# Half-size products for the first feed-forward matrix in 15 of 18 blocks, one pair's score seats from pair 10 on, and TensorE transposes for the first four pairs

## The chip, the core and the metric

The kernel runs on one core of a Trainium2 chip. The metric is the device time of one execution in microseconds (us). Engines: PE is TensorE (matmuls), PEld its weight loads, DVE VectorE, ACT ScalarE, POOL GpSimd, SP the engine that issues most DMAs. A matmul multiplies a stationary operand (`lhsT`, the weights, loaded by PEld) with a moving one (`rhs`) and writes to PSUM. A float32 matmul stands in the trace as two passes, each a weight load and a MATMUL, so the instruction counts of the profile are twice those of the program.

## The reference, cut to what matters

```python
# q, k, v: (8 batches, 8 heads, 576, 64); tau a scalar
scores = scale * q @ k.T
scores = where(scores >= max(scores) - tau, scores, -1e9)
attn = exp(scores - max(scores)); attn = attn / (sum(attn) + 1e-9)
x = (attn @ v), heads side by side            # (4608 tokens, 512)
h = x @ w_in                                  # (512 x 2048)
g = h * sigmoid(1.702 * h)
out = g @ w_out                               # (2048 x 512), float32
```

## The kernel before

**Attention.** Two heads make a pair `n`; there are 32 pairs, four to a batch. `load_qk` and `load_v` bring a pair in by DMA, `prep` (L504) turns q and k on DVE. `scores` (L514) makes nine tiles of 64 keys on PE, in bursts of four 64x64 quadrants; `keep` (L531) copies each from PSUM on ACT; `in_groups` (L537) takes maxima of groups on DVE, `over_tiles` and `over_halves` join them, and a row of thresholds is spread over the partitions, from most pairs by a DMA through DRAM (`turn_rows`, `row_out` L630, `row_in` L639; `BY_DMA` names the pairs), else by DVE (`spread_max` L618). Then, tile after tile, `sub` (L645, DVE), `mask` and `exps` (L651, L655, ACT). `values` (L666, PE) multiplies with v; the sums of the exponentials come from PE for the first five pairs (`sums_by_pe`) and from `in_groups` with an addition for the rest, their reciprocals again over DRAM (`turn_sums`, `sums_out`, `sums_in`). `place_x` (L768, DVE) scales the result into `xT`, the transposed input of the feed-forward part. The score tiles of a pair keep their place in SBUF (their seats) from `keep` to `values`; there are seats for two pairs, `s_m` and `s_t`. From pair 8 on (`JOINT = 7`, counted from 0) `values` of pair n-2 and `scores` of pair n alternate on PE tile by tile in one run, each new tile taking the seat that the old one leaves.

**Feed-forward.** 18 blocks of 256 tokens. Blocks 1 and 2 (`PLAIN = 2`) are done plainly together (`mm1_0` L823, `mm2` L805). In blocks 3 to 14 `mm1` (L783) makes the first product in 64 matmuls of 128x128 weights by 256 columns; `tanh` (L792, ACT) and `gelu` (L795, DVE) follow; the second product is made of seven half-size products instead of eight (`product` L974), with operand sums on POOL (`s_sums`, `s_last`) and seven results joined by DVE (`read` L996). Blocks 15 to 18 (`TAIL`) go two at a time through `two_blocks`: there the first product also is seven half-size products (`product1` L888: 112 matmuls of 256 columns for two blocks), read out by DVE (`read1` L904) into `hs`, and the weight sums (`w_sum` L862) are made on DVE and POOL when all pairs are placed.

**Order.** No hardware queue decides the order: `task` records every operation with its engine, a cost, a rank, what it comes after and which buffers it takes and gives; `run_in_order` plays these tasks through a list scheduler while the program is built and emits each engine's instructions in that order, which is then fixed. Pairs have low ranks and go on PE as soon as they are ready; feed-forward tasks (`LAST`) fill the rest. Pair n may not start before feed-forward task 16(n-6) has run:

```python
        gate = per_pair * (n - LEAD)
        ...
        after = [ffn[gate]] if gate >= 0 and ffn else []
```

`EARLY`, `SECOND`, `LATER` and `CV` are offsets added to the ranks. PSUM: `psA` has three slots of two banks (scores, values, and the odd products of `two_blocks`), `psM` two single banks (feed-forward).

Of the kernel before, what the change touches and what calls it, by code (L numbers as in the profile page):

```python
# [21 lines left out]
P = 128  # L22
# [10 lines left out]
def kernel(  # L33
# [84 lines left out]
    minus = const.tile([P, 2, KT], FP32, name="minus")  # L118
    own_row = const.tile([P, QB // 2], FP32, name="own_row")
# [8 lines left out]
    limits = {"psA": 3, "psM": 2, "s_m": 8, "s_t": 2, "io": 2, "hs": 2, "osb": 2, "xT": NXT, "mb": 1,  # L128
              "raw0": 1, "raw1": 1, "qkT0": 1, "qkT1": 1, "v_m0": 1, "v_m1": 1, "w64_0": 1, "w64_1": 1, "row": 1, "row_s": 1, "rc": 1}
    for x in ("raw0", "raw1", "qkT0", "qkT1", "mb"):  # L130
# [6 lines left out]
        "exps": 11.43,  # L137
        "in_groups": -31.63,
        "keep": -11.23,
        "load_qk": 20.14,  # L140
        "load_v": 19.9,
        "mask": 171.06,
        "one_row": -45.66,
        "over_halves": -1.59,
        "over_tiles": -20.68,
        "place_x": -28.05,
        "prep": -4.32,
        "row_in": 9.72,
        "row_out": -14.48,
        "scores_run": -28.58,  # L150
        "spread_max": 3.58,
        "spread_sums": 14.71,
        "sub": 178.85,
        "sums_by_pe": 312.21,
        "turn_rows": -14.38,
        "values": -19.56,
        "w_sum": -20.0,
    }
    SECOND = {
        "exps": 6.76,  # L160
        "in_groups": 291.18,
        "keep": 29.15,
        "load_qk": 165.77,
        "load_v": 335.03,
        "mask": 337.17,
        "one_row": -25.48,
        "over_halves": -20.33,
        "over_tiles": 311.35,
        "place_x": 0.09,
        "prep": -16.41,  # L170
        "row_in": 205.66,
        "row_out": 181.09,
        "scores_run": 21.47,
        "spread_sums": -6.66,
        "sub": 17.25,
        "sums_by_pe": 334.76,
        "sums_in": -21.09,
        "sums_out": 5.24,
        "turn_rows": 184.92,
        "turn_sums": -18.91,  # L180
        "values": -19.14,
    }
    LATER = {
        "exps": 208.23,
        "in_groups": 342.52,
        "keep": -7.99,
        "load_qk": 197.24,
        "load_v": -11.46,
        "mask": 344.07,
        "over_halves": -19.6,  # L190
        "over_tiles": 19.84,
        "place_x": 181.51,
        "prep": 208.92,
        "row_in": -6.54,
        "row_out": -30.86,
        "scores_run": -0.21,
        "sub": 200.03,
        "sums_in": 338.15,
        "sums_out": 7.27,
        "turn_rows": 167.17,  # L200
        "turn_sums": 343.8,
        "values": -25.3,
        "x_sum": -9.1,
    }
    CV = {
        "cv_end": 5.42,
        "cv_low": -24.3,
        "cv_power": 173.78,
        "cv_power2": -24.9,
        "cv_round": -14.9,  # L210
        "cv_whole": -11.38,
        "load_w": 330.13,
# [123 lines left out]
    TWICE = ()  # L336
# [12 lines left out]
    for tag, size, bufs in (  # L349
        ("s_m", 2 * S, 8), ("s_t", S, 2), ("raw0", S, 1), ("raw1", S, 1), ("qkT0", S, 1),  # L350
        ("qkT1", S, 1), ("mb", S, 1), ("rc", S, 1), ("v_m", NK * 2 * D, 2),
    ):
        room[tag] = [(end + x * size, size) for x in range(bufs)]
        end += bufs * size
# [12 lines left out]

    def seat_scores(n, t):

        if t < NKT and n in APART:  # L370
            return home(n, "s_m", f"s_m{t}")
        if n >= JOINT:
            tag, o, size = held[n, t] = held.pop((n - 2, t))
            return arena2[:, o : o + size]
        tag = "s_m" if t < NKT else "s_t"
        o, size = room[tag].pop(0)
        held[n, t] = tag, o, size
        return arena2[:, o : o + size]
# [13 lines left out]
    def load_qk(n, which, queue, h):  # L392
        b, hp = divmod(n, NPAIR)
        src = (q, k)[which]
        t = home(n, f"raw{which}")
        blocks = t.rearrange("p (c d) -> p c d", d=32)
# [7 lines left out]
        raws[n, which] = t  # L404

    def load_v(n):
        b, hp = divmod(n, NPAIR)
        t = seat("v_m", n % 2).rearrange("p (h j d) -> p h j d", j=NK, h=2)
        for h in range(2):
            for c in range(2):  # L410
                nc.sync.dma_start(
                    out=t[ts(c, KT), h],
                    in_=v[b, 2 * hp + h].rearrange("(k j) d -> k j d", k=KT),
                )
        vs[n] = t
# [90 lines left out]

    def halves(ap):
        return ap.rearrange("p (c s) -> p c s", c=2)

    def scores(n, j):  # L510
# [8 lines left out]
        if j == NK - 1 and n not in TWICE:  # L519
            del mats[n, 0], mats[n, 1]  # L520
# [12 lines left out]
    def in_groups(n, t, op):  # L533

        if (n, op) not in stats:
            stats[n, op] = work.tile([P, NK * QB], FP32, name="part", tag="part", bufs=2)
# [6 lines left out]
    def over_tiles(n, op):  # L543

        r = work.tile([P, QB], FP32, name="red", tag="red", bufs=2)
# [7 lines left out]
    def over_halves(n):  # L553
# [7 lines left out]
        if n in TWICE:  # L561
            for x, y in ((0, 0), (1, 2), (2, 1), (3, 3)):
                nc.vector.scalar_tensor_tensor(
                    out=flat[0][ts(y, 32), 0:QB], in0=r[ts(x, 32)], scalar=gap[ts(x, 32)],
                    in1=o[ts(x, 32)], op0=ALU.subtract, op1=ALU.max,
                )
            return
# [14 lines left out]

    def row_blocks(n):

        nc.vector.transpose(out=flat[1], in_=flat[0])
        mb = home(n, "mb")[:, 0:SH]
        nc.vector.tensor_tensor(
            out=mb.rearrange("p (g i) -> p g i", i=32),
            in0=flat[1].unsqueeze(1).to_broadcast([P, QB // 2, 32]),
            in1=own_row.unsqueeze(2).to_broadcast([P, QB // 2, 32]), op=ALU.mult,  # L590
        )
        mbs[n] = mb

    def again(n, j):
        ps = psA.tile([P, 2, 512], FP32, name="ps", tag="ps")
        for first in (True, False):
            for h in range(2):
                for c in range(2):
                    if first:
                        left = mats[n, 1][ts(h, D), ts(j, KT)]  # L600
                        right = mats[n, 0][ts(h, D), ts(c, SH)]
                    else:
                        left, right = minus[ts(h, D), c, :], mbs[n][ts(h, D), :]
                    nc.tensor.matmul(
                        ps[ts(c, KT), h, 0:SH], lhsT=left, rhs=right, start=first, stop=not first,
                    )
        if j == NK - 1:
            del mats[n, 0], mats[n, 1]
        pss[n, j] = ps

    def mask_one(n, j):
        nc.scalar.activation(
            out=sT[n, j // 2][:, j % 2], in_=pss.pop((n, j))[:, :, 0:SH], func=AF.Prelu, alpha=STEEP
        )
# [122 lines left out]
    def sums_in(n):  # L737
        rc, row = seat("rc"), rcs.pop(n)
# [7 lines left out]
    def spread_sums(n):  # L746
# [3 lines left out]
        rc = seat("rc")  # L750
# [77 lines left out]
    def gelu_0(j):  # L828
# [8 lines left out]
    TAIL = NBLK - 4  # L837
    WQ = NDC // 2 * HF * P
    gx_o = 4 * WQ
    xs_o = gx_o + N_G  # L840
    hs_o = xs_o + 3 * NDC // 2 * BLK
    assert hs_o + 8 * BLK <= end and BLK == 2 * P
    wc = [arena2[:, ts(x, WQ)].rearrange("p (c f) -> p c f", f=HF * P) for x in range(4)]
    gs = [g, arena2[:, ds(gx_o, N_G)].rearrange("p (f j t) -> p f j t", f=2, t=BLK)]
    xsum = [
        arena2[:, ds(xs_o + x * 2 * BLK, 2 * BLK)].rearrange("p (c t) -> p c t", c=2)
        for x in range(3)
    ]
    hs = [
        arena2[:, ds(hs_o + x * 4 * BLK, 4 * BLK)].rearrange("p (f h t) -> p f h t", f=2, h=2)  # L850
        for x in range(2)
    ]
# [3 lines left out]
        (wc[0], wq[1][0], wq[1][1], ALU.add), (wc[1], wc[0], wq[0][0], ALU.subtract),  # L856
        (wc[2], wq[0][0], wq[1][0], ALU.subtract), (wc[3], wq[0][1], wc[1], ALU.subtract),
    ]

    def w_sum(x, k, engine):  # L860
        o, a, b = (y[:, :, ts(k, 2 * P)] for y in W_SUMS[x][:3])
        engine.tensor_tensor(out=o, in0=a, in1=b, op=W_SUMS[x][3])  # L862

    def x_quarter(blk, d, h):
        return xTs[blk + h][:, ts(d, 2), :]
# [7 lines left out]

    BANK_OF = ("psA", "psM", "psA", "psM", "psA")
    places = {}

    def product1(blk, j, x):
        b11, b12, b21, b22 = (x_quarter(blk, d, h) for d in range(2) for h in range(2))
        left, right = (
            (wq[0][0], b11), (wq[0][1], b21), (wc[1], xsum[1]), (wc[2], b12),  # L880
            (wq[1][1], xsum[2]), (wc[0], xsum[0]), (wc[3], b22),
        )[x]
        if BANK_OF[(7 * j + x) % 5] == "psA":
            places[j, x] = psA.tile([P, 2, 512], FP32, name="ps", tag="ps")[:, 0, 0:BLK]
        else:
            places[j, x] = psM.tile([P, BANK], FP32, name="ops", tag="mo")[:, 0:BLK]
        for c in range(2):
            nc.tensor.matmul(  # L888
                places[j, x], lhsT=left[:, c, ts(j, P)], rhs=right[:, c, :],
                start=(c == 0), stop=(c == 1),  # L890
            )

    def read1(j, x):
        (c11, c12), (c21, c22) = ([hs[j % 2][:, f, h, :] for h in range(2)] for f in range(2))
        ps = places.pop((j, x))
        if x == P1:
            nc.scalar.copy(out=c21, in_=ps)
            return
        sums = {
# [585 lines left out]
```

## Time and profile before

| what | us |
|---|---|
| median of 3 runs (1298.23 to 1299.97) | 1299.56 |
| the profiled execution, its time | 1299.66 |
| its span, first to last instruction | 1297.9 |
| PE busy within the span | 1252.3 |
| DVE / ACT / POOL busy | 986.2 / 677.7 / 240.6 |

The span is the time between the first and the last instruction of the profiled execution; 1.8 us of its time lie outside it. Busy is the union of an engine's instructions; a row of instructions that overlap counts the overlap once. The prediction below reads the profile in stretches, since the kernel has a start (first loads and weight conversion), a long middle in which attention and feed-forward alternate, and a tail of feed-forward alone from about 1078 us on.

### The profile page before, as it was taken

To read this page: it belongs to the slowest core of one execution; us is meant where nothing else is said; L and a number is where in the kernel's file an instruction comes from. 1 tells how busy PE (TensorE), PEld (TensorE's weight loads), DVE (VectorE), ACT (ScalarE), POOL (GpSimd) and SP (SyncE) were. 2 spreads that over 40 slices of the span, in tenths; PEclk is the share of its full clock that TensorE was granted. 3 is DMA by queue.
4 is the path that set the end of the run, shared out by engine and by line. 5 is a ranking of instruction groups with operands and counts; after the bars stand their busy time and mean duration, and the time that the engine had idled before them with its cause. 6 is when DMAs were issued, how large, how long until landed. Compare 5 with 4: busy or idle time off the path is not lost. (4 is left out here: it accounts for less than half of the span.)

```text
span 1297.9 us, 22745 instructions
## 1 busy us (share of the span) xinstructions
PE 1252.3 (96%) x9128; PEld 972.9 (75%) x9128; DVE 986.2 (76%) x1553; ACT 677.7 (52%) x878; POOL 240.6 (19%) x277
## 2 busy tenths in 40 slices
PE   4689999999999999999999999999999999999998
PEld 2347854577777888777777788887777788888887
DVE  6999987989988787777887878777778863652642
ACT  5999876686755545454555555544546540210210
POOL 1000101131030303021120312030302117120120
PEclk8799999999999999999999999999999999999999
DMA  9735356183222222222122222222221100000000
GB/s 243 179 76 146 109 132 115 58 144 84 72 55 56 56 72 56 72 47 64 55 48 63 47 63 56 72 56 73 55 61 35 51 27 17 1 1 33 1 1 33
DMA packets 190825, 87.01 MB, mean 67 GB/s; under 512 B 159872, under 2 KB 170112, under 8 KB 190720
## 3 DMA queue, kind: packets, MB, share of 16 engines
q1 hardware_dynamic: 182560, 78.08, 23.7%
q0 software_dynamic: 5792, 7.19, 3.1%
q8 instruction: 71, 1.16, 0.4%
q10 hardware_dynamic: 2368, 0.30, 0.2%
q14 instruction: 34, 0.28, 0.1%
HBM read 71.63 MB, written 9.70 MB: 63 GB/s over the span
## 5 line engine op out<-in xcount | busy, mean ns | idle before, releaser
L537 DVE TRANSPOSE_TENSOR_REDUCE part<-arena 128x36 f32<-128x1152 f32 (+1 forms) x295 | 358.1, 1236 | 48.1 <-ACT arena L531 38.2
L783 PE MATMUL hps<-xT,w_in 128*128 128x256 f32 x1536 | 338.9, 381 | 2.9 <-DVE arena L795 2.9
L783 PEld LDWEIGHTS hps<-xT,w_in 128*128 128x128 f32 x1536 | 291.8, 191 | 48.9 <-issue 5.3
L651 ACT ACTIVATE arena<-arena 128x1152 f32<-128x1152 f32 (+1 forms) x160 | 169.4, 1059 | 127.4 <-DVE arena L645 127.2
L531 ACT COPY arena<-ps 128x576 f32<-128x576 f32 x288 | 171.0, 642 | 111.8 <-PE ps L514 108.9
L645 DVE TENSOR_TENSOR arena<-arena 128x1152 f32<-128x1152 f32 (+1 forms) x158 | 202.1, 1320 | 19.2 <-DMA arena<-row 19.1
L974 PE MATMUL ops<-w_out,arena 128*128 128x256 f32 x896 | 202.7, 381 | 1.7 <-DVE arena L795 1.6
L655 ACT ACTIVATE arena<-arena,shift,scl 128x1152 f32<-128x1152 f32 (+1 forms) x160 | 200.1, 1250 | 4.0
L974 PEld LDWEIGHTS ops<-w_out,arena 128*128 128x128 f32 x896 | 169.1, 190 | 29.4 <-DVE arena L795 3.8
L514 PE MATMUL ps<-arena 64*64 64x288 f32 x2304 | 172.1, 413 | 19.5 <-DVE neg L1035 9.1
L940 POOL TENSOR_TENSOR arena<-arena 128x256 f32<-128x256 f32 x56 | 51.8, 925 | 647.1 <-DVE arena L795 544.0
L666 PE MATMUL pv<-arena 64*64 64x288 f32 x2176 | 159.6, 407 | 0.0
L974 PE MATMUL ops<-arena 128*128 128x256 f32 x672 | 150.6, 380 | 0.0
L792 ACT ACTIVATE th<-hps 128x512 f32<-128x512 f32 x112 | 66.1, 590 | 161.7 <-PE hps L783 148.2
L514 PEld LDWEIGHTS ps<-arena 64*64 64x64 f32 x2304 | 85.4, 135 | 81.5 <-ACT arena L531 17.5
L974 PEld LDWEIGHTS ops<-arena 128*128 128x128 f32 x672 | 127.3, 190 | 19.3 <-issue 2.2
L666 PEld LDWEIGHTS pv<-arena 64*64 64x64 f32 x2176 | 81.0, 133 | 54.7 <-issue 8.8
L996 DVE SCALAR_TENSOR_TENSOR osb<-ops,osb 128x256 f32<-128x256 f32 x98 | 39.6, 415 | 94.2 <-PE ops L974 88.0
L795 DVE SCALAR_TENSOR_TENSOR arena<-th,hps 128x512 f32<-128x512 f32 x96 | 64.3, 670 | 37.4 <-ACT th L792 37.0
L908 ACT ACTIVATE th<-arena 128x512 f32<-128x512 f32 x32 | 20.3, 635 | 72.6 <-DVE arena L904 72.6
L953 POOL TENSOR_TENSOR arena<-arena 128x512 f32<-128x512 f32 x28 | 37.4, 1340 | 106.7 <-PE ops L974 106.6
L805 PE MATMUL ops<-w_out,arena 128*128 128x512 f32 x128 | 56.8, 598 | 0.0
(118 smaller groups left out, 1072.8 us busy)
## 6 DMA issues: line engine op xcount, KB each, us to landing
arena<-in_v_dram SPq DMA_DIRECT2D x128, 144.0 KB
arena<-in_q_dram SPq DMA_DIRECT2D x128, 72.0 KB
out_dram<-osb SPq DMA_DIRECT2D x36, 256.0 KB
arena<-in_k_dram SPq DMA_DIRECT2D x124, 72.0 KB
arena<-row SPq DMA_DIRECT2D x48, 144.0 KB
arena<-row_s SPq DMA_DIRECT2D x48, 144.0 KB
w_out<-in_moe_w_in_dram SPq DMA_DIRECT2D x12, 512.0 KB
arena<-in_moe_w_out_dram SPq DMA_DIRECT2D x12, 512.0 KB
```

The costliest lines, as they stand in the source:

```text
L514: nc.tensor.matmul(ps[ts(c, KT), h, 0:SH], lhsT=mats[n, 1][ts(h, D), ts(j, KT)], rhs=mats[n, 0][ts(h, D), ts(c, SH)], start=True, stop=True,)
L531: nc.scalar.copy(out=sT[n, t][:, u], in_=pss.pop((n, j))[:, :, 0:SH])
L537: nc.vector.tensor_reduce(out=stats[n, op][:, t * 2 * QB : min(2 * t + 2, NK) * QB], in_=sT[n, t].rearrange("p u h (g d) -> p (u h g) d", ...
L645: engine.tensor_tensor(out=s, in0=s, in1=mbs[n].unsqueeze(1).to_broadcast(list(s.shape)), op=ALU.subtract)
L651: nc.scalar.activation(out=s, in_=s, func=AF.Prelu, alpha=STEEP)
L655: nc.scalar.activation(out=s, in_=s, func=AF.Exp, scale=scl, bias=shift)
L666: nc.tensor.matmul(o[c][ts(h, D), 0:SH], lhsT=left(j, h)[ts(c, KT)], rhs=sT[n, t][ts(c, KT), u, h, :], start=(j == 0), stop=(j == NK - 1),)
L783: nc.tensor.matmul(hidden[j][:, ts(f, BLK)], lhsT=w_in[:, c, ds((f * HF + j) * P, P)], rhs=xTs[blk][:, c, :], start=(c == 0), stop=(c == N ...
L792: nc.scalar.activation(out=ths[j], in_=hidden[j], func=AF.Tanh, scale=GELU_SCALE / 2)
L795: nc.vector.scalar_tensor_tensor(out=g[:, :, j, :], in0=two(ths.pop(j)), scalar=1.0, in1=two(hidden.pop(j)), op0=ALU.add, op1=ALU.mult,)
L805: nc.tensor.matmul(acc[i], lhsT=g0[:, j, ts(i, P)], rhs=w_out[:, j, :], start=(j == 0), stop=(j == NFC - 1),)
L974: nc.tensor.matmul(banks[blk][k][:, ts(o, HM)], lhsT=left[:, j, :], rhs=right[:, j, :], start=(j == 0), stop=(j == HF - 1),)
```

## The change

1. **First product.** `FIRST7 = 3`: blocks 4 to 18, each by itself, make the first product of seven half-size products (`seven`). A half-size product has 128 tokens as its moving operand. Sums of partial products are kept in PSUM: P6, P7 and P4 accumulate on P1's bank, P3 on P5's; ACT copies the bank out between them (`keep1`), DVE adds P2, P5 and P3 to the copies (`add1`). Block 3 alone still uses `mm1`. `two_blocks`, `read1`, `hs` and the second copy of `g` are gone. The weight sums are made in the middle of the kernel (`w_sums`): ACT copies one operand (`w_copy`), a POOL DMA adds the other (`w_plus`).
2. **Seats.** From pair 10 on (`SINGLE = 9`) there are seats for one pair only; the other half of the arena holds the weight sums and `xsum`. `values` of pair n-1 and `scores` of pair n alternate, and `keep` waits also for the additions of the pair before.
3. **Thresholds.** `BY_DMA` ends at pair 9; from pair 10 on `spread_max` spreads them on DVE.
4. **First four pairs.** q and k are loaded in longer rows and turned by PE (`turn_in`), then copied from PSUM by ACT (q) and DVE (k).
5. All rank offsets differ, and each load has one of its own (`L_RANK`); the POOL sums of the second product go in halves of 512 columns, the subtraction (`s_minus`) apart.

```diff
-    BY_DMA = (0, 1, *range(3, NP))
+    BY_DMA = (0, 1, *range(3, SINGLE))
...
+    SINGLE = 9
+    TURNED = (0, 1, 2, 3)
...
+    def ahead(n):
+        return n - 1 if n >= SINGLE else n - 2
...
+        if n in TURNED:
+            rows = src[b, 2 * hp + h]
+            if which:
+                queue.dma_start(out=t[ts(h, D), :], in_=rows.rearrange("(k j) d -> k (j d)", k=KT))
+                return
+            queue.dma_start(
+                out=t[:, 0 : 4 * P].rearrange("p (c d) -> p c d", d=P)[:, :, ts(h, D)],
+                in_=rows[0 : 4 * P].rearrange("(c p) d -> p c d", p=P),
+            )
+            queue.dma_start(out=t[ts(h, D), 4 * P : S], in_=rows[4 * P : S])
+            return
...
+    def turn_in(n, which):
+        raw = raws.pop((n, which))
+        bank = pss[n, -1 - which] = psA.tile([P, 2, 512], FP32, name="ps", tag="ps")
+        ps = bank.rearrange("p a b -> p (a b)")
+        x = 0 if which else 4 * P
+        for o in range(0, x, P):
+            nc.tensor.transpose(ps[:, ds(o, P)], raw[:, ds(o, P)], eye)
+        for o in range(x, S, D):
+            for h in range(2):
+                nc.tensor.matmul(
+                    ps[ts(h, D), ds(o, D)], lhsT=raw[ts(h, D), ds(o, D)],
+                    rhs=eye[ts(h, D), ts(h, D)], start=True, stop=True,
+                )
...
-    TAIL = NBLK - 4
+    FIRST7 = 3
...
+    W_SUMS = [
+        (wc[0], wq[1][1], wq[1][0], 1.0), (wc[1], wc[0], wq[0][0], -1.0),
+        (wq[1][0], wq[0][0], wq[1][0], -1.0), (wc[2], wq[0][1], wc[1], -1.0),
+    ]
...
+    def w_copy(x, c):
+        o, _, b, sign = W_SUMS[x]
+        nc.scalar.activation(out=o[:, c, :], in_=b[:, c, :], func=AF.Copy, scale=sign)
+
+    def w_plus(x):
+        o, a = W_SUMS[x][:2]
+        nc.gpsimd.dma_start(out=o, in_=a, accum_op=ALU.add)
...
     def x_quarter(blk, d, h):
-        return xTs[blk + h][:, ts(d, 2), :]
+        return xTs[blk][:, ts(d, 2), ts(h, HT)]
...
+        o = bank1(x, y)
+        for j in range(4):
+            for c in range(2):
+                nc.tensor.matmul(
+                    o[:, ts(j, HT)], lhsT=left[:, c, ts(4 * y + j, P)], rhs=right[:, c, :],
+                    start=(x in (P1, P2, P5) and j + c == 0), stop=(j + c == 4),
+                    skip_group_check=True,
+                )
...
+    def keep1(x, y):
+        f, h = {P1: (0, 0), P6: (0, 1), P7: (1, 1)}[x]
+        nc.scalar.copy(out=quarter(y, f, h), in_=four(bank1(x, y)))
+
+    def add1(x, y):
+        f, h = {P2: (0, 0), P5: (1, 1), P3: (0, 1)}[x]
+        o = quarter(y, f, h)
+        nc.vector.tensor_tensor(out=o, in0=four(bank1(x, y)), in1=o, op=ALU.add)
...
+    def seven(blk):
...
+        for x in (P1, P2, P6, P5, P7, P4, P3):
+            for y in range(2):
...
+                if x in (P6, P7, P4):
+                    after = after + [keeps[{P6: P1, P7: P6, P4: P7}[x], y]]
+                if x == P3:
+                    after = after + [adds[P5, y]]
+                ffn.append(task(
+                    "PE", FFU, LAST, product1, blk, x, y, after=after,
+                    take=("psM",) if x == P1 else ("psA",) if x in (P2, P5) and y == 0 else (),
+                    give=("xT",) if x == P3 and y else (),
+                ))
...
         def copied(n, r, j, a):
-            copies.append(task("ACT", 0.55, r, keep, n, j, after=[a] + copies[-1:], give=("psA",)))
+            before = sumsd[n - 1][j // 2 :][:1] if n >= SINGLE else []
+            copies.append(task(
+                "ACT", 0.55, r, keep, n, j, after=[a] + copies[-1:] + before, give=("psA",)
+            ))
```

## The prediction

> **What bounds the kernel now.** I read the page's busy line and chain first, then the span in four stretches, the waits of PE, and single passes in the timeline of PE.
>
> ```profile
> PE 1252.3 (96%) x9128; PEld 972.9 (75%) x9128; DVE 986.2 (76%) x1553; ACT 677.7 (52%) x878; POOL 240.6 (19%) x277
> ...
> PE 17%; DVE 0%; issue 0%
> ```
>
> PE is busy in all but 45.6 us, and the chain that ended last is PE alone. By stretches (PE, PEld, DVE, ACT, POOL busy; then the granted clock):
>
> ```profile
> 0.00:108.60 108.60, 71.21 (x1009) 39.19 (x1009) 93.06 (x147) 91.77 (x121) 9.09 (x33) 0.91 0.64 157
> 108.60:260.00 151.40, 151.40 (x1035) 96.03 (x1032) 134.35 (x214) 116.60 (x155) 18.43 (x30) 1.00 0.45 115
> 260.00:1078.30 818.30, 813.84 (x6093) 648.39 (x6092) 664.10 (x1004) 442.81 (x550) 166.31 (x169) 1.00 0.26 61
> 1078.30:1298.00 219.70, 215.84 (x999) 189.35 (x997) 94.68 (x191) 26.56 (x53) 46.74 (x46) 1.00 0.03 13
> ```
>
> 37.4 of the 45.6 idle us lie before 108.6, where the feed-forward part starts; from there on PE waits 8.3 us in 1189. So work taken from PE after 108.6 comes off the end, as long as nothing else gets in its way. The waits agree: those on ACT's exponentials and on the turned q and k are in the start.
>
> ```profile
> PE den L666 <- ACT arena L655: 17.9, 8, 13.4
> PE ps L514 <- DVE neg L1035: 9.1, 1, 9.1
> PE ps L514 <- DVE arena L504: 6.1, 1, 6.1
> ...
> PE hps L783 <- DVE arena L795: 2.9, 2, 2.2
> ```
>
> **The first product.** A pass of 256 columns costs PE 32 passes from 607.47 to 614.38, 216 ns each (the row's mean of 380 overlaps):
>
> ```profile
> 607.47 7.07 PE L974 MATMUL ops<-arena 128*128 128x256 f32 x32
> 614.38 3.62 PE L974 MATMUL ops<-w_out,arena 128*128 128x256 f32 x16
> ```
>
> Removed: 704 matmuls of L783 (768 less the 64 of block 3) and all 224 of L888, two passes each: 1856 x 0.216 = 400.9 us. Added: 15 blocks x 14 tasks x 8 = 1680 matmuls of 128 columns, 3360 passes. None like it is in the trace. From below it costs half of 216, 108 ns. From above, 192: a weight load of 128x128 stands as 190 ns, begins 2 ns after the pass before it, and no pass could be shorter if it had to be over. Which end is nearer, one late load tells:
>
> ```profile
> 362.34 0.63 PE L783 MATMUL hps<-xT,w_in 128*128 128x256 f32 x2
> ...
> 362.49 0.19 PEld L783 LDWEIGHTS hps<-xT,w_in 128*128 128x128 f32 x1 [0.17 <-DVE arena L795]
> ...
> L783 PE MATMUL hps<-xT,w_in x7: 379/379/414, 361.5 to 362.8; 128*128 128x256 f32 x7
> ```
>
> This load waited for DVE and began 0.15 us after the pass at 362.34. The pass behind it lasted 414 instead of 379, so it was 35 ns late and in effect began 216 + 35 = 251 ns after 362.34: some 100 ns after its load began, not 190. A load therefore is about hidden under a half-size pass. I take 109 ns: 3360 x 0.109 = 366.2. Net **-34.7** (-38.0 at 108, +244 at 192).
> By the Trainium skill (TensorE: Matmul & The Clock Gate, Back-to-back issue gap), a stream of weight load and matmul pairs at 128 columns runs at about 81 ns a matmul where an isolated one takes 56, 25 ns more; an estimate by it is 3360 x 0.025 = 84 us on top, 1361 in all. This speaks against the change; the trace shows nothing of the kind at 256 columns, and no run here yet shows 128.
>
> **The middle: PE against DVE.** The program's order on PE is fixed when it is built, and in the middle it now repeats two gaps between the runs of `values` and `scores`: 208 short passes and 14 long (25.7 us), then 98 long and 16 short (22.9). With two runs of 8.9 (591.55 to 600.46) a cycle of two pairs and one block takes PE 66.4 us; before it was 73. DVE in that time:
>
> ```profile
> 473.00:546.00 73.00, 73.00 (x543) 58.68 (x543) 57.31 (x88) 38.43 (x49) 13.14 (x14) 1.00 0.24 57
> ...
> L795 DVE SCALAR_TENSOR_TENSOR arena<-th,hps 128x512 f32<-128x512 f32 x96 | 64.3, 670 | 37.4 <-ACT th L792 37.0
> L904 DVE TENSOR_TENSOR arena<-ps,arena 128x256 f32<-128x256 f32 x68 | 27.5, 421 | 15.9 <-PE ps L888 15.0
> L913 DVE SCALAR_TENSOR_TENSOR arena<-th,arena 128x512 f32<-128x512 f32 x32 | 25.5, 800 | 2.6 <-ACT th L908 2.6
> L618 DVE STREAM_TRANSPOSE arena<-red 128x576 f32<-128x576 f32 x1 | 0.8, 778 | 0.0
> ```
>
> Three such windows mean 58.0 us. Off it goes the block's share, 8 `gelu` x 0.67 and 7 `read` x 0.40 = 8.2, times 32/31 blocks: 49.6 for two pairs. Thresholds on DVE add per pair 0.78 (L618) and two more `fold` at 0.28 and one joining operation at 0.24, and drop two at 0.30 and `turn_rows` at 0.21: +0.8. A block now needs 6 `add1` (512 columns; between L795's 0.67 and twice L904's, 0.84; I take 0.67, the same size), 6 `gelu` out of SBUF at 0.80, 2 at 0.67, 4 `x_sum` at 0.41 (the 256-column `place_x`), 7 `read`: 14.6. Together 51.2 + 14.6 = 65.8 of 66.4 us. DVE goes from 79% to 99%, and nearly level with PE. The trace bears 98% for 65 us, from 292 to 357, with PE never waiting:
>
> ```profile
> 292.10:324.50 32.40, 32.40 (x334) 23.20 (x327) 31.59 (x55) 20.57 (x29) 5.62 (x5) 1.00 0.34 84
> 324.50:357.00 32.50, 32.50 (x254) 25.78 (x254) 32.27 (x45) 23.38 (x28) 2.00 (x4) 1.00 0.28 72
> ```
>
> I take 97% as what DVE can reach: 65.8 / 0.97 = 67.8, 1.4 us over PE in each of 10.5 cycles: **+14** (0 to +52, below). With one set of seats a run also waits for the last exponential of the pair before. From a run's start: last full maximum 10.2 (L537 ends 601.7), then `place_x` 0.9, tail 0.7, joining 1.8, spreading 0.8, first `sub` 1.4, four tiles at 2.44 on ACT (39.00 to 41.44 to 43.88) and a tail of 1.5: 27.1. In the short gap's 31.8 this has 4.7 to spare. In the long gap ACT's order puts four `keep1` and two `tanh` at 0.6 within the chain and DVE's two `add1` and a `gelu`: 32.7 of 34.6. What is late first is `add1` of P3: it frees the `psA` slot for the next run, and behind it on PE stands that whole run. `keep`'s new wait (sums of the pair before, DVE) holds the other copies on ACT and through `psA` the scores; the sums are over before it, since DVE does them first.
>
> **The start.** q and k of four pairs came in rows of 128 bytes (72 KB a DMA, 576 rows, two a head and operand: 18432 packets, of 22462 in the first 60 us); now 256 bytes for q, 2304 for k, some 5100. Thresholds of pair 1 took from 20.5 to 37.0 to return, against 5 us later on (606.5 to 611.6). Eight `prep` (0.72) leave DVE, four copies join DVE and four ACT (0.64); ACT also has about 0.7 more of conversion before the feed-forward part. The turns, 16 of 128 columns (0.109 to 0.43 each) and 160 small passes (at most 0.06 each, the 64x288 row), 3 to 17 us of PE, lie under 37.4 idle us; without that cover they would cost that much. ACT was idle 16.8 us of 108.6; that is the most that can come forward, and its 3.3 extra us the loss if nothing does. I take **-4** (-17 to +3).
>
> **Weight sums and queues.** `w_sums` puts eight ACT copies (1.04 each, the 128x1024 row) and four POOL DMAs of 1 MB (9 to 10 us to land, as L934) into 250 to 330. The four like DMAs at L934 came with 2.9 us of waits of PE there; I take **+2** (0 to +6). SP loses 92 issues for thresholds (L630, L639: 96 to 4) and POOL none; POOL's sums are as many columns as before. Second product and tail are four blocks of 48.6 us PE each as before (L974 unchanged, two blocks 24.2 + 24.2 in L888 against 48.8), under DVE's 14.6 a block.
>
> **Sum.** 1297.9 - 34.7 - 4 + 14 + 2 = 1275.2; with the 1.8 outside the span **1277**. The profiled execution (1299.66) is within 0.1 of the median, so it needs no correction.
>
> **Rivals.**
> - *No lag, quicker start.* DVE's 99% is too high since it counts operations that waited at 60 ns more than dense ones (two L537 take 2.63, one alone 1.38); the start gives 10. 1297.9 - 34.7 - 10 + 1 + 1.8 = **1256**.
> - *Some lag more*, 2.5 to 3.5 us a cycle: 1289 to 1299.
> - *DVE and the single seats set the pace.* POOL slows DVE (`sub` means 1.42 where most last 1.35), the long gap's DVE work, summed in its order up to P3's `add1`, is 36.4 us from the run's start against PE's 34.6, and PE can't use the short gap's slack since its order is fixed. At 5 us a cycle +52: **1315**, slower. It decides from 3.5 us on ((34.7 + 4 - 2) / 10.5). For it: the sums above; against it: 98% without a wait at 292 to 357.
> - *The weight load shows* in short passes, halfway to 192: 3360 x 0.041 = 138 more, **1415**; from 116 ns on nothing is gained. For it: the 190 of the rows. Against it: the late load. The rule quoted above is of this kind.
>
> **How the numbers follow.** Forecast 0.55 (own range 1264 to 1289), quicker 0.17, more lag 0.09, DVE's pace 0.13, weight load 0.06. 0.2%, 2.6 us, is what a measurement of this kernel can tell. Faster: 0.55 + 0.17 + 0.06 of the more-lag case = 0.78; same 0.04, where the two lag cases meet 1299.6; slower 0.12 + 0.06 = 0.18. The range leaves out a part of the quick case below (0.05), and above most of the DVE case (0.09) and the weight load (0.06): 1254 to 1305.
>
> **What would show it.** In the profile after: rows of 128 columns on PE in x16 pieces 1.74 us apart; PE busy near 1225 us; the first `mm1_0` pass at about 104; DVE at 95% or more from 300 to 1000; PE waits on L902 or on `ps` by one to two us a cycle. The prediction is wrong in its first step if short passes start 116 ns or more apart, in its second if PE waits more than 3 us a cycle or not at all.

## The result and the profile after

The changed kernel takes 1342.31 us (median of 4 runs, 1340.58 to 1346.92) against 1299.3 for the kernel before on the same chip: 1.0333 times, 95% interval 1.0315 to 1.0351. It is slower by 43 us where 1277 was forecast. The profiled execution took 1346.92, with a span of 1345.1.

The busy line and the chain of the page of after:

```profile
PE 1257.9 (94%) x10808; PEld 1013.1 (75%) x10808; DVE 1041.2 (77%) x1592; ACT 730.8 (54%) x964; POOL 212.1 (16%) x189
...
PE 52%; DVE 28%; ACT 9%; DMA 6%; issue 4%; POOL 1%; SPq 0%; DVEq 0%; ACTq 0%; POOLq 0%
```

Now 28% of the span goes through DVE and 9% through ACT: PE is no longer the only bound. (The chain of the kernel before held PE alone, but could be followed back over 17% of its span only; that PE was the bound there rests on its 8.3 idle us after 108.6.) The same four stretches as in the prediction, cut at the same events (start of the feed-forward part, end of the first two blocks, last `values`); columns as there:

```profile
0.00:113.10 113.10, 82.17 (x1185) 47.72 (x1185) 91.15 (x139) 92.93 (x125) 8.08 (x25) 0.86 0.58 146
113.10:271.80 158.70, 151.00 (x965) 93.66 (x962) 140.36 (x228) 119.20 (x155) 18.50 (x30) 0.98 0.47 117
271.80:1140.90 869.10, 825.17 (x7314) 685.41 (x7312) 750.36 (x1126) 485.00 (x626) 144.70 (x102) 0.99 0.24 54
1140.90:1345.00 204.10, 199.54 (x1356) 186.36 (x1352) 59.34 (x101) 33.72 (x60) 40.82 (x32) 1.00 0.04 14
```

In the third stretch PE stands idle for 44 us, in a stretch where it had been idle for 4.5. What it waited for there, by the waits of PE (total us, times, longest):

```profile
PE ops L970 <- DVE osb L992: 24.8, 10, 5.3
PE den L657 <- ACT arena L646: 17.3, 3, 11.8
PE ps L545 <- ACT arena L562: 9.4, 6, 6.6
PE ps L883 <- DVE arena L902: 6.3, 8, 0.8
```

The second and most of the third line belong to the start and to the first two blocks. The first line is new: the second product (`product` L970) waits for DVE to read the bank it is to write again (`read` L992).

The half-size product itself does nearly what was forecast. In PE's timeline 32 passes of 128 columns start 3.58 us before the next 32, 111.7 ns each:

```profile
584.74 3.74 PE L883 MATMUL ps<-xT,w_in 128*128 128x128 f32 x32
588.32 3.74 PE L883 MATMUL hps<-arena 128*128 128x128 f32 x32
```

With such spacings (111.7 ns for 128 columns, 216 for 256, 429 for 512, 61 for the 64x288 quadrants) the passes of each stage can be summed as work; what the stage lasts beyond it is lost on PE, by waiting or by a lower clock. This table is worked out in that way from the passes of the two traces:

| stage | before: work + lost | after: work + lost |
|---|---|---|
| to the first feed-forward pass | 61.1 + 47.5 | 67.7 + 45.4 |
| to the end of blocks 1 and 2 | 149.5 + 2.7 | 145.1 + 13.6 |
| to block 3's second product | 36.4 + 5.8 | 45.1 + 10.7 |
| to the last scores | 718.9 + 9.2 | 727.6 + 58.6 |
| to the last values | 32.9 + 0.7 | 23.8 + 3.3 |
| to the end | 228.1 + 5.1 | 198.6 + 5.7 |
| sum | 1226.8 + 71.0 = 1297.9 | 1207.9 + 137.3 = 1345.1 |

Work fell by 18.9 us (25.6 by the shorter passes, 6.6 given back to the turns of q and k), losses rose by 66.3, of which 49.4 in the steady middle. The execution that was profiled is 4.6 us longer than the median, so the stages add up to a little more than the 43 us.

One place in the middle shows how. First DVE, then POOL, then PE, each from its own timeline (start, length):

```profile
553.33 3.12 DVE L588 TENSOR_SCALAR fold<-red,gap 32x18 f32<-32x18 f32 x4
556.49 0.24 DVE L599 SCALAR_TENSOR_TENSOR red<-red,gap,fold 128x18 f32<-128x18 f32 x1
556.64 0.42 DVE L992 SCALAR_TENSOR_TENSOR osb<-ops,osb 128x256 f32<-128x256 f32 x1
```

```profile
553.36 1.27 POOL L950 TENSOR_TENSOR arena<-arena 128x512 f32<-128x512 f32 x1 [5.59 <-PE ops L970]
555.15 1.26 POOL L950 TENSOR_TENSOR arena<-arena 128x512 f32<-128x512 f32 x1 [0.52 <-PE ops L970]
```

```profile
551.39 3.62 PE L970 MATMUL ops<-arena 128*128 128x256 f32 x16
557.20 3.04 PE L970 MATMUL ops<-w_out,arena 128*128 128x256 f32 x13 [2.19 <-DVE osb L992]
```

Four subtractions on 32x18 elements (`fold`, L588), which elsewhere take 0.95 us together (at 585.27, for one), take 3.12 here, while two POOL sums run. The next `read` stands behind them on DVE, and PE waits 2.19 us for it, about as long as the four were late. From 500 to 1106 us, DVE operations of four kinds that overlap a POOL `TENSOR_TENSOR` by more than a tenth last much longer than their like that don't (a count over the raw trace; mean ns, number):

| operation of DVE | clear of POOL | under POOL |
|---|---|---|
| fold copy, L714 | 168 (37) | 831 (24) |
| fold subtract, L588 | 228 (52) | 821 (12) |
| `x_sum`, two operands in SBUF, L861 | 397 (19) | 1147 (13) |
| `sub` of a whole tile, L636 | 1352 (57) | 2062 (7) |
| reduction L577 / transposes L719 / reciprocal L718 | 436 / 211 / 266 | 436 / 212 / 266 |
| `read` out of PSUM, L992 | 402 (54) | 401 (3) |

The excess of the first four rows is 38 us, 4.6 in each 72.5 us cycle of two pairs. In the kernel before, all such operations counted alike from 480 to 1023 us, it was 20 us, 2.6 a cycle; three in four of its POOL pieces have 256 columns and last 0.72 us instead of 1.27.

### The profile page after: what moved, and what is told of

The parts are those of the page before. It is cut to its first block, busy times and chain, and to the rows that moved or that the text cites. A ratio compares the mean times of both kernels' runs of the same rounds, so it can differ in the third digit from the quotient of the medians.

```text
span 1345.1 us, 25947 instructions
## 1 busy us (share of the span) xinstructions
PE 1257.9 (94%) x10808; PEld 1013.1 (75%) x10808; DVE 1041.2 (77%) x1592; ACT 730.8 (54%) x964; POOL 212.1 (16%) x189
## 4 chain that ended last, share of the span: by engine, by line
PE 52%; DVE 28%; ACT 9%; DMA 6%; issue 4%; POOL 1%; SPq 0%; DVEq 0%; ACTq 0%; POOLq 0%
PE ops L970 16%; PE hps L883 11%; PE ps L883 9%; PE pv L657 6%; DVE part L568 6%; PE ps L545 5%; DVE arena L636 4%; ACT arena L642 3%; ACT arena L646 3%; DVE fold L714 2%; DVE arena L914 2%; DVE fold L588 2%; DMA arena<-row 2%; DVE arena L902 2%; PE ops L796 2%
## 5 line engine op out<-in xcount | busy, mean ns | idle before, releaser
L568 DVE TRANSPOSE_TENSOR_REDUCE part<-arena 128x36 f32<-128x1152 f32 x295 | 360.0, 1238 | 58.3 <-ACT arena L562 49.4
L970 PE MATMUL ops<-w_out,arena 128*128 128x256 f32 x1024 | 240.0, 389 | 25.3 <-DVE osb L992 24.6
L970 PEld LDWEIGHTS ops<-w_out,arena 128*128 128x128 f32 x1024 | 196.3, 195 | 61.6 <-POOL arena L950 22.3
L636 DVE TENSOR_TENSOR arena<-arena 128x1152 f32<-128x1152 f32 (+1 forms) x158 | 197.9, 1301 | 13.3 <-DMA arena<-row 12.8
L970 PE MATMUL ops<-arena 128*128 128x256 f32 x768 | 173.4, 381 | 3.0 <-POOL arena L941 2.8
L970 PEld LDWEIGHTS ops<-arena 128*128 128x128 f32 x768 | 144.6, 190 | 27.1 <-POOL arena L941 4.4
L897 ACT COPY arena<-hps 128x512 f32<-128x512 f32 x90 | 51.3, 576 | 160.5 <-PE hps L883 160.5
L902 DVE TENSOR_TENSOR arena<-ps,arena 128x512 f32<-128x512 f32 x90 | 60.4, 679 | 94.3 <-PE ps L883 65.1
L909 ACT ACTIVATE th<-arena 128x512 f32<-128x512 f32 x90 | 56.4, 630 | 123.1 <-DVE arena L902 122.7
L883 PEld LDWEIGHTS hps<-xT,w_in 128*128 128x128 f32 x960 | 111.4, 192 | 5.9 <-issue 3.9
L883 PE MATMUL hps<-xT,w_in 128*128 128x128 f32 x960 | 114.7, 276 | 0.8 <-DVE osb L992 0.8
L992 DVE SCALAR_TENSOR_TENSOR osb<-ops,osb 128x256 f32<-128x256 f32 x112 | 44.5, 409 | 68.0 <-PE ops L970 66.7
L914 DVE SCALAR_TENSOR_TENSOR arena<-th,arena 128x512 f32<-128x512 f32 x90 | 60.0, 675 | 14.8 <-ACT th L909 14.7
L883 PE MATMUL ps<-xT,arena 128*128 128x128 f32 x480 | 58.2, 277 | 6.3 <-DVE arena L902 6.3
```

The costliest lines, as they stand in the source:

```text
L568: nc.vector.tensor_reduce(out=stats[n, op][:, t * 2 * QB : min(2 * t + 2, NK) * QB], in_=sT[n, t].rearrange("p u h (g d) -> p (u h g) d", ...
L636: engine.tensor_tensor(out=s, in0=s, in1=mbs[n].unsqueeze(1).to_broadcast(list(s.shape)), op=ALU.subtract)
L883: nc.tensor.matmul(o[:, ts(j, HT)], lhsT=left[:, c, ts(4 * y + j, P)], rhs=right[:, c, :], start=(x in (P1, P2, P5) and j + c == 0), stop= ...
L902: nc.vector.tensor_tensor(out=o, in0=four(bank1(x, y)), in1=o, op=ALU.add)
L909: nc.scalar.activation(out=four(ths[y, f, h]), in_=final1(y, f, h), func=AF.Tanh, scale=GELU_SCALE / 2)
L914: nc.vector.scalar_tensor_tensor(out=quarter(y, f, h), in0=four(ths.pop((y, f, h))), scalar=1.0, in1=final1(y, f, h), op0=ALU.add, op1=ALU ...
```

## The experiments

Theory S: these stalls on DVE, through the order fixed on PE, make the loss of the middle. Rival P: the plan packed the order too tightly for the chip in any case. All times are medians beside runs of the kernel before on the same chip (1299.9 to 1300.6).

**No POOL sums.**

```diff
     def s_sums(k):
...
-        nc.gpsimd.tensor_tensor(out=u1, in0=a21, in1=a22, op=ALU.add)
-        nc.gpsimd.tensor_tensor(out=u2, in0=u1, in1=a11, op=ALU.subtract)
+        return
```

(`s_minus` and `s_last` likewise.)

> The changed kernel without the operand sums of the second product on POOL (s_sums, s_minus, s_last emit nothing, so the second product multiplies unsummed operands and the output is not the reference's); order of every engine otherwise as it was. Theory S (small SBUF-to-SBUF operations of DVE stand still while a POOL tensor_tensor runs, 4.6 us a cycle of two pairs, and DVE's lateness reaches PE): the folds fall to their clear durations, copy 0.17 (from 0.50 mean) and subtract 0.23 (from 0.35), x_sum to 0.40 (from 0.79); a cycle falls from 72.5 to about 68 us and the time from 1342 to about 1295 (1285 to 1310). Rival P (the order on PE was packed for shorter handoffs than the chip has, whatever POOL does): the folds get shorter but a cycle stays above 71.5 and the time above 1330.

Measured: 1301.43, 41 us less than the changed kernel; a cycle takes 68.8 (36.8 and 32.0) instead of 72.5. The same 420 us of the middle, 640 to 1060, first in after, then in this run:

```profile
640.00:1060.00 420.00, 401.40 (x3590) 337.53 (x3589) 373.36 (x559) 235.80 (x305) 65.27 (x48) 0.99 0.20 48
```

```profile
640.00:1060.00 420.00, 414.99 (x3813) 349.75 (x3811) 358.49 (x583) 246.72 (x320) 0.00 (x0) 1.00 0.22 51
```

PE's idle time falls from 18.6 to 5.0 us, while DVE does more instructions (583 against 559) in less time. The groups of the folds in that window, after and this run (busy us, mean ns):

```profile
L714 DVE COPY fold<-red 32x18 f32<-32x18 f32 x44 | 20.7, 470 | 0.8
L588 DVE TENSOR_SCALAR fold<-red,gap 32x18 f32<-32x18 f32 x48 | 15.9, 331 | 0.9
```

```profile
L588 DVE TENSOR_SCALAR fold<-red,gap 32x18 f32<-32x18 f32 x48 | 10.9, 228 | 1.0
...
L714 DVE COPY fold<-red 32x18 f32<-32x18 f32 x48 | 8.1, 168 | 0.9
```

Theory S stands, P falls as the main cause. This run also takes away every wait for the sums themselves, but those are small: of PE's waits in the changed kernel 2.8 us are put down to L941 and 0.7 to L945. The weight loads have 22.3 us put down to L950, POOL's last sum; yet the product that waits at 557.20 (P7) does not read that sum, and in the next run, with pieces of 256 columns, P7 starts at 816.93 while that sum runs until 817.96.

The middle still loses 21.3 us, 12 more than in the kernel before, and something is left for P. The only waits of PE from 345 to 1100 us:

```profile
PE ps L883 <- DVE arena L902: 6.3, 8, 0.8
```

Once a cycle the second half of P3 waits for an `add1` that starts only when the first half of P3 has ended (at 784.32, for one). The summed passes put 7.6 of the 12 us there, 2.3 into eight places where PE's weight loads wait 0.3 us for `keep1`, and 1.7 into one wait for `read` at 337.55.

**POOL sums in 256 columns.**

```diff
-        nc.gpsimd.tensor_tensor(out=u1, in0=a21, in1=a22, op=ALU.add)
...
+        for i in (2 * k, 2 * k + 1):
+            a11, a21, a22, u1, u2 = (y[:, ts(i, 2), :] for y in (qas[0][0], qas[1][0], qas[1][1], s1, s2))
+            nc.gpsimd.tensor_tensor(out=u1, in0=a21, in1=a22, op=ALU.add)
...
```

> The changed kernel with the POOL sums cut into pieces of 256 columns, as the kernel before had them, same columns in all. Theory S: a stall lasts at most one piece (0.72 instead of 1.27 us), so about half of the 4.6 us a cycle comes back: cycle about 70.2, time about 1320 (1312 to 1330). Rival P: cycle 72.5 and 1342 within 4. If a stall does not end with a piece but with the whole sum, nothing changes either.

Measured: 1322.97; a cycle takes 70.3. The folds lie between:

```profile
L714 DVE COPY fold<-red 32x18 f32<-32x18 f32 x48 | 13.2, 274 | 0.9
L588 DVE TENSOR_SCALAR fold<-red,gap 32x18 f32<-32x18 f32 x48 | 13.1, 273 | 1.0
```

A stall ends with the POOL instruction, not with the whole sum: the longest copy was 0.68 here, 1.22 in after. None, 256 and 512 columns give 1301, 1323 and 1342. (The kernel before had its last sum in 512 columns; here all four are cut.)

**A wider gap between the runs.**

```diff
         gate = per_pair * (n - LEAD)
+        if n > 19:
+            gate = max(gate, 226 + 16 * (n - 19))
```

> The changed kernel with a later gate from pair 21 on: some 18 feed-forward tasks (30 us of PE work) move from the tail into the middle, between the runs. The planner's own plan is as long as before to 1 us (1253.7 against 1252.8). Theory S and rival P both have PE waiting in the middle for DVE with feed-forward work left for the tail, so both expect the time to fall. If DVE's pace for two pairs stays, 72.5 for attention and the old share of feed-forward, the added tasks bring 0.5 us of DVE each: gain 18 x (1.68 - 0.5) = 21, time about 1321 (1308 to 1332). If the loss lies in fixed handoffs at each run rather than in DVE's load, nothing is gained: 1342 within 5.

Measured: 1327.43, 15 us less, 6 short of the 21 expected. The middle loses 45.9 instead of 58.6 though it holds 30 us more of PE work (757.7 against 727.6). So PE waited in the middle with work at hand that the plan had put into the tail.

**Half-size first products in the last four blocks only.**

```diff
-    FIRST7 = 3
+    FIRST7 = 14
...
-    SINGLE = 9
+    SINGLE = 29
```

> The changed kernel with half-size first products only from block 15 on and single seats and thresholds on DVE only from pair 30 on (the start with its turned pairs, rank offsets and POOL pieces of 512 columns stay). Blocks 4 to 14 use whole first products as the kernel before. Theory: the start is as in the changed kernel (first feed-forward pass at about 113, first two blocks over at about 272), the middle keeps before's pace of 35.9 us a pair, and the time is about 1325 (1312 to 1340), between the two kernels; the wait of PE for DVE in the middle is gone. Rival (the new rank offsets and POOL's longer pieces alone slow the middle): a pair takes 36.5 or more and the time is above 1340.

Measured: 1345.25, a miss of 20 us. The middle went as expected: 35.9 us a pair, 12.8 lost in 742. That the new rank offsets or POOL's pieces slow the middle by themselves is out. But this program's order, which the planner makes another one from the early pairs on, lost 26.5 us in the first two blocks and 16.2 up to block 3's second product, 30.4 of it in five waits of PE for `keep`, the longest 12.3. The early loss therefore isn't made by half-size products.

**Folds on ACT.**

```diff
+    def swap(o, s):
+        for x in range(4):
+            nc.scalar.copy(out=o[ts(x ^ 1, 32)], in_=s[ts(x, 32)])
...
+            a = task("DVE", 0.23, r, lower_max, n, after=[a])
+            a = task("ACT", 0.8, r - 4.0, swap_max, n, after=[a])
+            a = task("DVE", 0.18, r, join_max, n, after=[a])
```

> The changed kernel, from pair 10 on, with the eight fold copies of a pair (four in over_halves, four in turn_sums) on ACT instead of DVE; POOL's sums stay, in 512 columns. Theory S: DVE loses the 16 operations a cycle that stood 2.75 us a cycle under POOL, and their own 3.2 us; what remains under POOL is sub and x_sum, 1.8 us a cycle. Handing to ACT and back costs two semaphores a fold. A cycle falls from 72.5 to about 69, the time from 1342 to about 1306 (1298 to 1318). If ACT's copies stand still under POOL as DVE's do, they last 0.8 in the mean instead of 0.2, and half of that gain is lost. Rival (the longer POOL pieces hurt by lateness of the sums themselves, not by holding DVE): 1335 or more.

Measured: 1324.06, half of the expected gain. ACT's copies do not stall (204 ns in the mean). But the shifted order brings `x_sum` under POOL, in this run's groups (means around 400 when clear):

```profile
L887 DVE TENSOR_TENSOR arena<-xT,arena 128x256 f32<-128x256 f32 x12 | 16.1, 1346 | 0.2
L887 DVE TENSOR_TENSOR arena<-xT 128x256 f32<-128x256 f32 x6 | 8.7, 1442 | 0.0
```

To take away the operations that stall is not to take away the stalls; another operation of the kind meets the same POOL sum.

**No additions by DMA to the weight sums.**

```diff
     def w_plus(x):
-        o, a = W_SUMS[x][:2]
-        nc.gpsimd.dma_start(out=o, in_=a, accum_op=ALU.add)
+        return
```

> The changed kernel without the four DMAs of 1 MB that add the second operand of the weight sums (w_plus emits nothing, the ACT copies stay, so the half-size products use wrong sums). Theory D (those DMAs delay the rows of sums and thresholds, which took 9.4 and 5.8 us to come back at 287.8 and 328.3 and held place_x on DVE): the stretch from the end of the first two blocks to block 3's second product loses 5 to 6 us instead of 10.7, the first two blocks' own loss of 13.6 stays (their late rows lie before these DMAs), the time falls by 4 to 8, to about 1336. Rival (the row's own trip, v's load or the order on the queues make it late): within 2 us of 1342.

Measured: 1334.51, 7.8 us less. Up to block 3's second product 4.6 are lost instead of 10.7, the first two blocks still lose 13.6. The wait of `place_x` for its sums, from 113 to 345 us, in after and in this run:

```profile
DVE xT L759 <- DMA arena<-row_s: 10.1, 2, 5.9
```

```profile
DVE xT L759 <- DMA arena<-row_s: 0.6, 1, 0.6
```

The row issued at 287.83 in after came back at 297.31, here the one issued at 284.31 was back by 291.46.

**Three edits together** (256 columns, wider gap, folds on ACT).

> The changed kernel with three edits together: POOL sums in 256 columns, the later gate from pair 21 on, the folds on ACT from pair 10 on. Singly the first gave 19 us and the second 15. If stalls under POOL and the tight order are two sides of one shortage of DVE time, the gains overlap: with DVE below 60 us of 70 a cycle, PE should wait about 10 us in the whole middle, and the time is about 1290 (1282 to 1302). If they add up in full with the 36 expected of the folds: 1275. If the handoffs to ACT dominate: 1310 or more.

Measured: 1308.88, 19 above the 1290 expected. From 370 to 1110 us PE now loses some 21 us, no wait longer than 2.5; the rest of what is lost lies before: 43.3 in the start, 13.4 and 12.0 in the next two stages.

**The kernel before without POOL sums.**

```diff
     def s_last(k, w):
...
-        nc.gpsimd.tensor_tensor(out=u, in0=a12, in1=u, op=ALU.subtract)
+        return
```

> The kernel before without the operand sums of the second product on POOL (s_sums and s_last emit nothing; the output is not the reference's). Theory S says that the same stalls stand in the kernel before, 2.0 us a cycle, but that DVE's spare time takes them up, PE being the limit: folds fall to 0.17 and 0.23, DVE's busy time by some 15 us, and the time stays within 3 us of 1299. Rival: if the time falls by 10 us or more, the stalls reached PE there too and were part of the time before.

Measured: 1302.28, ratio 1.0015 (1.0006 to 1.0025). Folds of the kernel before, then of this run, 480 to 1023 us:

```profile
L723 DVE COPY fold<-red 32x18 f32<-32x18 f32 x62 | 14.2, 229 | 1.2
L557 DVE TENSOR_SCALAR fold<-red,gap 32x18 f32<-32x18 f32 x30 | 10.0, 335 | 1.0
```

```profile
L723 DVE COPY fold<-red 32x18 f32<-32x18 f32 x64 | 10.8, 168 | 1.2
L557 DVE TENSOR_SCALAR fold<-red,gap 32x18 f32<-32x18 f32 x30 | 6.9, 229 | 1.0
```

DVE's busy time falls from 986.2 to 957.3, twice what was expected, and the time doesn't. The stalls were there before the change; they cost nothing while PE alone was the bound.

**The planner told what was measured.** The three edits, and:

```diff
-            t_ready.append(task("POOL", 1.0, T_RANK, t_plus, x, after=after, lag=9.0))
+            t_ready.append(transfer("DMW", 7.6, task("POOL", 1.0, T_RANK, t_plus, x, after=after), 1, lag=1.5))
...
-                    "PE", FFU, LAST, product1, blk, x, y, after=after,
+                    "PE", 1.787, LAST, product1, blk, x, y, after=after,
...
-            xd.append(task("DVE", 0.34, LAST - 1.0, x_sum, blk, x, after=(xd[-1:] or xs) + last1))
+            xd.append(task("DVE", 0.5, LAST - 1.0, x_sum, blk, x, after=(xd[-1:] or xs) + last1))
```

(`w_plus` as `t_plus`; the rank offsets and the gate's slope are other numbers.)

> The three edits of the run with 256-column POOL sums, later gate and ACT folds, and the planner told what the traces showed: the eight 1 MB DMAs stand in its plan as transfers of 7.6 us that slow the rows, a half-size product costs 1.787 us, DVE's operations and x_sum cost what they lasted under POOL, the first load lands 3.5 us later; offsets of the ranks chosen anew for that plan, and one end of the gate's slope with them. All engines do the same work as in that run, in another order. If the 13.4 us lost in the first two blocks and the 12 in block 3 are an order planned on too short row trips, they fall to about 5 and 5, the middle stays at 25 and the time falls from 1309 to about 1285 (1275 to 1298), faster than both kernels. If they come from the work itself (more on ACT, DMAs in each other's way), the time stays above 1303.

> As order a, with another set of offsets that the plan rates equal (1263.8 against 1263.1) but with the last pairs' runs some 17 us later in the plan. If the plan now holds what the chip does, both orders take the same to about 8 us, near 1285; if they differ by more than 15, the plan still lacks something that decides.

Measured: order a 1293.14, ratio to the kernel before 0.994 (0.9926 to 0.9955): faster than both kernels, and than the kernel before by 0.6%. Order b 1301.01, 16 above the 1285 expected. Order a's first two blocks and the stage to block 3's second product:

```profile
110.80:259.50 148.70, 148.57 (x965) 93.27 (x962) 137.46 (x218) 117.31 (x150) 18.56 (x30) 1.00 0.47 114
259.50:301.80 42.30, 38.57 (x273) 30.50 (x272) 29.62 (x41) 29.24 (x40) 14.67 (x12) 0.96 0.83 142
```

Losses there are 3.6 and 6.0 us (order b: 6.4 and 7.0) with the same work on the same engines: the early loss was order. The two orders, which the plan rates equal to 0.7 us, differ by 7.9. Of the 9.6 between their profiled executions 6.8 lie in the start (first feed-forward pass at 110.8 and 117.6), the rest mostly in these two stages. The middle keeps 26 to 28 us of loss in both.

**Without turning on TensorE.** Order a with `TURNED = ()`, offsets chosen anew, twice.

```diff
-    TURNED = (0, 1, 2, 3)
+    TURNED = ()
```

> Order a with the first four pairs' q and k loaded in rows of 128 bytes and turned on DVE (prep) as in the kernel before; rank offsets chosen anew for the same planner. PE has 6.6 us less to do in the start. If turning on TensorE brings the start forward as its longer rows should, the feed-forward part starts later here, at about 117 instead of 110.8 (the plan has it 7.8 later), and the time is about 1301 (1296 to 1308). If the turns only swap idle time of PE for work, the feed-forward part starts at 108 to 112 and the time stays at 1293 within 4.

> As the run before, with another set of offsets of equal plan (1270.9 against 1271.0) and a planned start of the feed-forward part 3 us earlier. The two together tell what an order's luck is worth here: for the same verdict both should lie on the same side of 1297.

Measured: 1304.67 and 1299.93, feed-forward part from 120.5 and 114.9. Both lie above 1297, as the case for turning asked, but order b, which turns, took 1301.01. Between orders of equal plan lie 5 to 8 us, as much as between turning and not turning. What the turns are worth stays open.

## Why the prediction was wrong

From the forecast span of 1275.2 to the 1345.1 measured, the terms of the sum went wrong by: short passes 9.1, start 8.5, middle 35.4, weight sums and queues 13.8, end of the attention and tail 3.2.

- **The first product: mechanism right, size off.** Forecast 109 ns a pass and -34.7; measured 111.7 and 3360 x 0.1117 - 400.9 = -25.6. The rival of the weight load (116 ns and more) fell. By the 25 ns a matmul that the Trainium skill adds for pairs of load and matmul (TensorE: Matmul & The Clock Gate, Back-to-back issue gap) an estimate would be 109 + 25 = 134; the trace shows 111.7.
- **The middle: the step that failed.** The prediction put it as "I take 97% as what DVE can reach: 65.8 / 0.97 = 67.8, 1.4 us over PE in each of 10.5 cycles: **+14** (0 to +52, below)". DVE was busy 64.8 us a cycle, near the 65.8, but by luck: 4.6 of it were stalls under POOL that the estimate did not name, and without POOL's sums DVE takes 59.7, 6 less than estimated. DVE reached 89%, 64.8 of 72.5, and the lag did not come from its load divided by a reach: it came mostly at one place, where a `read` stands behind stalled folds and PE waits 2.4 us in most cycles. Without POOL's sums a cycle takes 68.8, 1.0 over the forecast's 67.8. The prediction's own sign against this step, PE waiting more than 3 us a cycle, came true (2.4, 0.8 and 0.5 in most cycles); it had looked for the waits at `add1` (L902), where they are 6.3 us in all against 24.8 at `read`. The 98% of the row from 292 to 357 came from a stretch with 7.6 us of POOL work and other operations beside it. In a cycle DVE waits 7.7 us, in the runs for `keep` and in the long gap for products, and in the short gap PE waits for DVE; with PE's order fixed, neither can be full. The case that came true was the rival "DVE and the single seats set the pace", given 0.13, with 1315 and 5 us a cycle; measured were 4.7 over 10.5 cycles, and it named POOL's drag on `sub` but not on the folds.
- **POOL's sums, costed at nothing.** The prediction's "POOL's sums are as many columns as before" was true and beside the point: 512-column pieces hold DVE's small operations nearly twice as long as 256-column ones did (831 ns a copy against 459 in the kernel before), and the cover that made this free, DVE's spare time, was what the change used up. Leaving the sums out gives 41 us, cutting them into 256 columns 19. The Trainium skill has the rule that the prediction passed over (SBUF — State Buffer, SBUF: two separate sides): VectorE and GpSimd share a pair of ports, which the operation that starts first takes whole, and the other "fully blocks"; it names DVE operations with two SBUF inputs or in a two-port mode. The trace agrees by kind of operation: copies and `x_sum` stretch from 168 to 831 and from 397 to 1147 ns, transposes, reductions and reads of PSUM do not.
- **The short gap's 4.7 us to spare** became a lack: that gap takes 35.7 to 36.4 from run to run in after against 31.8 of PE work, and 32.0 without POOL's sums. The long gap takes 36.8 in all of after and in the run without POOL sums, 2.2 over its 34.6; that is what is left of the forecast's lag.
- **The start**, forecast -4, was +4.5 in the profiled execution: 6.6 of turns on PE, less 2.1 of waits. The same start in the seven other runs with the same early order lies between 107.4 and 113.2, at 110.1 in the mean, so some 3 of the 4.5 are that execution's own. The forecast covered the turns by idle time but missed that the idle time which ends last, PE waiting for ACT's exponentials of the first pairs (17.3 us after, 17.9 before), isn't shortened by earlier loads.
- **Weight sums and queues**, forecast +2, were +15.8. Some 6 to 8 are the DMAs of `w_plus`, shown by leaving them out: the row queued beside 1 MB came back after 9.5 us, without them within 7.2. The rest is order: it went when the work was ordered anew. That new plan held these transfers, but other measured costs too, so that the short row trips of the old plan were the reason is not shown by itself. Which single late row costs what in the first two blocks wasn't tried.

The 28 us that the middle still loses in order a are settled in part only: PE waits 6.8 us for ACT's copies out of the bank (`keep1`, at most 0.9 each) and 5.1 for POOL's sums, 4.3 of it at once; some 9 the kernel before lost as well.

## What to carry to other kernels

Before using up an engine's spare time, list what that time was hiding: here stalls of DVE under POOL that were already in the trace of before, at no cost. Where an order is fixed at build time by a plan, its costs have to be those of the changed kernel, contention and long DMAs included; the same work in another order moved this kernel by 8 to 16 us. Time off the bounding engine comes off the end only up to where the next engine's idle stretches, not its mean load, stop fitting under it.

## What was not expected of the hardware

A DVE copy of 32x18 elements can last 1223 ns instead of 168, nearly as long as the POOL operation beside it, while the same copy on ACT stays at 205. The trace points to holding in the other direction too: a POOL piece of 512 columns, 1.27 us mostly, lasted 1.60 at 539.74, where a `gelu1` with both operands in SBUF had begun 0.22 us earlier, and 2.40 at 611.67 between two `sub`; no run was made to test this alone. After the wait of 5.31 us at 343.49 the next 16 passes of 256 columns stand as 5.71 us instead of 3.62, the granted clock from 341 to 347 us is 0.50, and over the whole middle it is 0.99 instead of 1.00: this wait of PE cost more than its length. Identical starts differed by 6 us in when the feed-forward part began.
